# A fused attention and MLP kernel on one core: the SP queue's transfers pinned to program order through the attention, and the weight staging moved to later slots

## The chip, the core and the metric

The kernel runs on one core of a Trainium2 chip. The core has five engines that run their own instruction streams: TensorE (PE in the profile; PEld is its weight load), VectorE (DVE), ScalarE (ACT), GpSimd (POOL) and SyncE (SP). In this kernel SP computes nothing: it only issues DMA transfers, one after the other, and each transfer then runs on the core's 16 DMA engines. A transfer that is issued waits, at the head of SP's stream, until the data that it reads is there, and everything behind it waits as well.

The metric is the time of one execution in microseconds (us). Lower is better.

## What is computed

All in float32, with a sequence of 2048 tokens of 512 channels, 32 heads of 16 channels, a sliding window of 256 keys, and a hidden layer of 1792:

```python
x  = A_x
xn = layernorm(x)
q, k, v = split(xn @ A_wqkv)                       # 32 heads of 16
p  = softmax(mask(q @ k.T * 16 ** -0.5))           # causal, the last 256 keys
s  = (p @ v) @ A_wo
g  = silu(gelu(layernorm(xn) @ B_w1 + B_b1) @ B_w2 + B_b2)
return x + s * g
```

To keep float32 precision in TensorE's reduced format, the kernel splits operands into a high and a low part and sums three products (hi*hi, hi*lo, lo*hi).

## The kernel before, in words

**The slots.** The attention works through eight groups `n` of four heads, and each group through 16 blocks of 128 tokens. One step of this is a slot `t`; the loop at line 717 runs t from -16 to 128 and writes out what each engine gets, in order. In slot t, `prob_block` (line 456) computes the probabilities of group t // 16, block t % 16, in two halves: scores into the PSUM tile `stb`, exp by ScalarE into `pt`, masking by GpSimd. `pv_step` (line 477) multiplies the block before with the values (into `zo`) and copies the result into `oraw`. Twelve slots ahead of the probabilities, `max_block` (line 415) computes the same scores once more (into `xy` and `zo`) to find each row's maximum by VectorE; after every fourth block `max_rows` (line 440) sends 4 blocks of maxima through HBM (`mT_d`) into a spare row of the projection tile. The first pair of `stb` matmuls of slot 0 starts at 72.49 us, and every slot up to 115 has two such pairs, which is how slots are counted in the trace: slot 8 starts at 95.86, slot 9 at 98.88, slot 12 at 107.30, slot 13 at 116.19, slot 84 at 329.13 us.

**The fill work.** Between these steps TensorE gets pieces of other matmuls (the `fills`): projections of later groups (`job_qk`, line 244, and pairs of them, `pair_qk`, line 300, run by `tandem`, line 371), values, and the first hidden tiles of the MLP. A projection (n, c) covers group n and the c-th 512 tokens. When it is finished, its raw result is copied to `pjr`, ScalarE rounds it to the high part `sh`, GpSimd subtracts to get the low part (back into `pjr`), and SP sends four copies of the high part and two of the low part into the tile `qk`, which `max_block` and `prob_block` read. The first block of (n, c) is due in slot 16 n + 4 c - 12. The high part is made in slot `max(t + 1 + 2 * (c % 2), 16 * n - 28 + 4 * c)`, where t is the slot in which the projection ended, and the low part in the next slot that `quiet` (line 335) allows. For (1, 2) that is: ended in slot 8, high and low part in slot 9, due in slot 12.

**What sets the order.** `at(t, ...)` (line 582) puts a step into the middle of slot t. The class `Ordered` (line 32) wraps each engine, and pins each instruction behind the one before it on its engine, for all engines but SP. SP's instructions are put in order by the compiler's scheduler, from its own estimate of when data is ready; it may issue a transfer earlier or later than the program has it.

**The staging.** The MLP's weights are copied from the inputs into scratch HBM tensors `w_d` by 16 transfers of 512 KB (`stage_in`, line 533), put into slots 22, 24, ... 52 at line 670. They depend on nothing, and are read from slot 91 on (`fetch`, line 538).

**The MLP.** After the attention the loop over four chunks of 512 tokens does the hidden layer, the second layer, the output projection and the gate. It isn't touched.

Of the kernel before, what the change touches and what calls it, by code (L numbers as in the profile page):

```python
# [31 lines left out]
class Ordered:  # L32


    def __init__(self, tc, name):
        self.tc, self.name = tc, name

    def __getattr__(self, what):
        issue = getattr(getattr(self.tc.nc, self.name), what)

        def issued(*args, **kwargs):
            r = issue(*args, **kwargs)  # L42
            if self.name != "sync" and hasattr(r, "ins"):
                self.tc.keep_in_program_order(r)
            return r
        return issued
# [3 lines left out]
def mixer_kernel(ctx, tc, x, wqk, wv, wo, w1, b1, w2, b2, out):  # L50
# [22 lines left out]
    def copy_rows(dst, src):  # L73
        nc.sync.dma_start(dst.bitcast(F32), src.bitcast(F32))
# [169 lines left out]
    def job_qk(n, c):  # L244

        box = []
        ops = [(kt, a, b) for kt in range(KT) for a, b in PASSES]
        if not n and not c:
            ops.sort(key=lambda o: o[2])
        sl = slice(512 * c, 512 * (c + 1))  # L250

        def mm(i):
            if i == 0:
                box.append(fill_bank())
            kt, a, b = ops[i]
            nc.tensor.matmul(box[0], wqs[n][:, a, kt], big[:, b, kt, sl],
                             start=(i == 0), stop=(i == len(ops) - 1))

        def send(src, qk, tt):
            copy_rows(slots[n % 2][tt:P:4, qk, :, sl], src[64 * qk: 64 * qk + 64])  # L260

        def finish():
            hi = sgp.tile([P, 512], F32R, tag="sh", name=f"sh_{n}_{c}", bufs=2)
            raw = t2.tile([P, 512], F32, tag="t2", name=f"pjr_{n}_{c}")
            lo = raw.bitcast(F32R)
            nc.scalar.copy(raw, box[0])

            def high():
                nc.scalar.copy(hi, raw)
                if n >= 2:  # L270
                    copy_rows(slots[n % 2][3:P:32, 0, :, sl], slots[n % 2][7:P:32, 0, :, sl])
                for qk, tt in ((1, 0), (0, 0), (1, 2), (0, 1)):
                    send(hi, qk, tt)

            def low():
                (nc.gpsimd if n else nc.vector).tensor_tensor(lo, raw, hi.bitcast(F32), op=ALU.subtract)
                send(lo, 1, 1)
                send(lo, 0, 2)

# [20 lines left out]
    def pair_qk(n, c):  # L300
# [11 lines left out]
        def finish(ps, t, copy):  # L312
            hi = sgp.tile([P, 512], F32R, tag="sh", name=f"sh_{n}_{c}", bufs=2)
            raw = t2.tile([P, 512], F32, tag="t2", name=f"pjr_{n}_{c}")
            lo = raw.bitcast(F32R)
            copy(raw, ps)

            def high():
                nc.scalar.copy(hi, raw)
# [5 lines left out]
            def low():  # L325
                nc.gpsimd.tensor_tensor(lo, raw, hi.bitcast(F32), op=ALU.subtract)
                send(lo, 1, 1)
                send(lo, 0, 2)

            free = max(t + 1 + 2 * (c % 2), 16 * n - 28 + 4 * c)  # L330
            at(free, high)
            at(quiet(free), low)
        return 3 * KT, mm, finish

    def quiet(t):
# [20 lines left out]
    def pair_h(f):  # L356
# [5 lines left out]
        def finish(ps, t, copy):  # L362
            raw = t2.tile([P, 512], F32, tag="t2", name=f"hr_{f}")
            copy(raw, ps)
            if f < 4:
                soon[f] = raw
            else:
                nc.sync.dma_start(h_d[f - 6], raw)
        return 3 * KT, mm, finish

    def tandem(t0, t1, one, two, mid=None, back=None):
# [68 lines left out]
    def max_rows(n, c):  # L440

        mt = mts.pop((n, c))
        mh = small.tile([P, 2, 2, 2, 4], F32R, tag="mh", name=f"mh_{n}_{c}")
# [2 lines left out]
        mT = small.tile([P, 32], F32, tag="mT", name=f"mT_{n}_{c}")  # L446
        nc.vector.transpose(mT, mh.rearrange("p a l i b -> p (a l i b)").bitcast(F32))
        rows = mT_d[n, c]
        nc.sync.dma_start(rows.rearrange("r (i t) -> i r t", i=4), mT)
        nc.sync.dma_start(slots[n % 2][3:P:32, 0, :, 512 * c: 512 * (c + 1)].bitcast(F32),  # L450
                          rows.rearrange("(h p b) t -> h p (b t)", h=4, p=2))


    pts = {}
# [22 lines left out]
    def pv_step(n, qb, also=()):  # L477
# [11 lines left out]
            outs[0] = sgp.tile([P, 512], F32, tag="or", name=f"oraw_{n}_{qb}", bufs=2)  # L489
        nc.scalar.copy(outs[0][:, P * (qb % 4): P * (qb % 4 + 1)], otb)  # L490
        if qb % 4 == 3:
            nc.sync.dma_start(oT_d[n // 2, n % 2::2, :, P * (qb - 3): P * (qb + 1)], outs[0])


    mlp = {}
# [86 lines left out]
    def at(t, fn, *args):  # L582
        plan.setdefault(t, []).append((fn, args))

    fetch_wqk(0)
    fetch_wv(0)
    xs[1] = load_x(1, XE, "x")
# [349 lines left out]
```

## Time and profile before

| | |
|---|---|
| median of 3 runs | 791.07 us (789.85 to 793.46) |
| the profiled execution | 793.06 us |
| its span, first to last instruction | 791.4 us |
| mean granted TensorE clock | 0.992 |
| busy: PE, PEld | 756.2 us (96%), 587.8 us (74%) |
| busy: DVE, ACT, POOL | 484.6 us (61%), 373.0 us (47%), 313.5 us (40%) |
| the attention's slots 0 to 128 | 72.5 to about 452 us |
| DMA moved in all | 90.46 MB, 38.7% of the 16 engines' time on SP's queue |

How to read the profile: `out<-in` names the tile that an instruction writes and those that it reads. A wait is written `engine tile <- what ended the wait`. In a timeline the columns are start, length, engine and operation, a count, and in brackets the idle time ahead of it with its releaser. In a table of windows they are the stretch, its length, the busy time of each engine (with the number of instructions), the granted clock, the share of the DMA engines' time, and GB/s. On SP, the length of a group of transfers is the time to issue them, not the time until they land; landing times stand in the chain of waits, as `DMA out<-in`. All lines read L42 because the wrapper `Ordered` issues everything.

### The profile page before, as it was taken

To read this page: it belongs to the slowest core of one execution; us is meant where nothing else is said; L and a number is where in the kernel's file an instruction comes from. 1 tells how busy PE (TensorE), PEld (TensorE's weight loads), DVE (VectorE), ACT (ScalarE), POOL (GpSimd) and SP (SyncE) were. 2 spreads that over 40 slices of the span, in tenths; PEclk is the share of its full clock that TensorE was granted. 3 is DMA by queue.
4 is the path that set the end of the run, shared out by engine and by line. 5 is a ranking of instruction groups with operands and counts; after the bars stand their busy time and mean duration, and the time that the engine had idled before them with its cause. 6 is when DMAs were issued, how large, how long until landed. Compare 5 with 4: busy or idle time off the path is not lost.

```text
span 791.4 us, 18507 instructions
## 1 busy us (share of the span) xinstructions
PE 756.2 (96%) x7420; PEld 587.8 (74%) x7420; DVE 484.6 (61%) x751; ACT 373.0 (47%) x626; POOL 313.5 (40%) x586
## 2 busy tenths in 40 slices
PE   5999989999999999999999999999999999999997
PEld 4887656676668887666676777688888888888886
DVE  5786757787777678888974558733445235532343
ACT  4733746767776676777877834321122111221111
POOL 4101646657656554767766744320112011120101
PEclk9999989999999999999999999999999999999999
DMA  8965545555445312465623282530123011210011
GB/s 285 297 182 156 177 130 169 151 136 131 97 97 125 89 45 85 106 188 157 185 82 125 79 293 83 172 106 14 54 80 107 14 41 40 81 54 13 27 54 66
DMA packets 55061, 90.46 MB, mean 114 GB/s; under 512 B 10496, under 2 KB 14848, under 8 KB 54976
## 3 DMA queue, kind: packets, MB, share of 16 engines
q1 hardware_dynamic: 54976, 89.29, 38.7%
q8 instruction: 58, 0.95, 0.5%
q14 instruction: 27, 0.22, 0.1%
HBM read 44.05 MB, written 25.95 MB: 88 GB/s over the span
## 4 chain that ended last, share of the span: by engine, by line
PE 79%; DVE 8%; ACT 5%; DMA 3%; issue 2%; POOL 2%; SPq 1%; DVEq 0%; ACTq 0%; POOLq 0%
PE acc L42 16%; PE fb L42 16%; PE h L42 15%; PE zo L42 11%; PE stb L42 7%; PE s L42 6%; PE xy L42 5%; ACT pt L42 3%; PE pv L42 2%; DVE xy L42 2%; DVE mt L42 2%; POOL pt L42 1%; DVE xnT L42 1%; DMA qk<-sh 1%; DVE gl L42 1%
## 5 line engine op out<-in xcount | busy, mean ns | idle before, releaser
L42 POOL TENSOR_SCALAR_AFFINE_SELECT pt<-pt 128x256 f32<-128x256 f32 x480 | 196.1, 433 | 179.4 <-ACT pt L42 178.1
L42 ACT ACTIVATE pt<-stb 128x768 f32<-128x768 f32 (+1 forms) x244 | 189.0, 774 | 61.6 <-PE stb L42 53.2
L42 DVE TENSOR_REDUCE mt<-xy 128x4 f32<-128x1024 f32 (+1 forms) x128 | 152.6, 1192 | 4.4
L42 PE MATMUL acc<-w,gh 128*128 128x512 f32 x432 | 133.5, 390 | 1.0 <-DVE gh L42 1.0
L42 DVE COPY_PREDICATED xy<-upper,zo 128x512 f32<-128x512 int32 x112 | 77.6, 693 | 76.7 <-PE zo L42 75.9
L42 PE MATMUL fb<-xnT,wqb 64*128 64x512 f32 (+1 forms) x696 | 120.4, 410 | 0.6 <-DVE xnT L42 0.6
L42 ACT ACTIVATE g<-h,b1s 128x512 f32<-128x512 f32 x44 | 30.4, 691 | 189.9 <-PE h L42 189.9
L42 DVE CAST gh<-g 128x512 fp32r<-128x512 f32 x52 | 27.5, 529 | 137.9 <-PE acc L42 125.2
L42 PE MATMUL zo<-pt,vt 128*17 128x128 f32 x2880 | 104.4, 276 | 2.1 <-DVE xy L42 1.6
L42 PE MATMUL stb<-qk 64*128 64x384 f32 (+1 forms) x488 | 97.1, 393 | 7.3 <-ACT pt L42 5.8
L42 PEld LDWEIGHTS zo<-pt,vt 128*17 128x17 f32 x2880 | 67.8, 97 | 39.5 <-issue 18.2
L42 PEld LDWEIGHTS acc<-w,gh 128*128 128x128 f32 x432 | 80.9, 188 | 18.7 <-DVE gh L42 2.2
L42 PE MATMUL h<-xnT 128*128 128x512 f32 x320 | 92.0, 389 | 0.0
L42 PE MATMUL acc<-w,gl 128*128 128x512 f32 x216 | 84.8, 392 | 1.1 <-DVE gl L42 1.0
L42 PEld LDWEIGHTS stb<-qk 64*128 64x128 f32 x488 | 45.8, 184 | 52.5 <-ACT pt L42 41.3
L42 PEld LDWEIGHTS fb<-xnT,wqb 64*128 64x128 f32 (+1 forms) x696 | 67.5, 190 | 8.5 <-DVE xnT L42 1.0
L42 PEld LDWEIGHTS h<-xnT 128*128 128x128 f32 x320 | 60.1, 188 | 12.4
L42 PE MATMUL xy<-qk 64*128 64x256 f32 (+2 forms) x536 | 61.6, 304 | 6.6 <-DMA qk<-pjr 3.9
L42 PEld LDWEIGHTS xy<-qk 64*128 64x128 f32 x536 | 44.8, 187 | 17.0 <-issue 6.6
L42 PE MATMUL h<-yh,xnT 128*128 128x512 f32 x160 | 55.8, 389 | 0.0
L42 ACT COPY oraw<-zo 128x128 f32<-128x128 f32 x128 | 34.3, 268 | 39.0 <-PE zo L42 35.0
L42 POOL TENSOR_TENSOR or<-or,w 128x512 f32<-128x512 f32 x16 | 21.5, 1350 | 73.0 <-DMA or<-oT_d 65.1
(115 smaller groups left out, 962.7 us busy)
## 6 DMA issues: line engine op xcount, KB each, us to landing
qk<-sh SPq DMA_DIRECT2D x128, 128.0 KB
qk<-pjr SPq DMA_DIRECT2D x64, 128.0 KB
oT_d<-oraw SPq DMA_DIRECT2D x32, 256.0 KB
w_d<-in_w_dram SPq DMA_DIRECT2D x14, 512.0 KB
x<-in_x_dram SPq DMA_DIRECT2D x16, 256.0 KB
or<-oT_d SPq DMA_DIRECT2D x16, 256.0 KB
w<-rden_d SPq DMA_DIRECT2D x16, 256.0 KB
xo<-in_x_dram SPq DMA_DIRECT2D x16, 256.0 KB
```

The source lines that it names most:

```text
L42: r = issue(*args, **kwargs)
```

## The change

Four things change.

- **SP is pinned in the loop.** `Ordered` gets a switch; for SP it is on through the slot loop, so each transfer there is pinned behind the one before it in the program. Before and after the loop SP is free as it was.
- **Each transfer gets a place.** A new `behind(t, ...)` puts a step at the very end of slot t. The sends of a projection go behind the slot in which its high or low part is made; the two transfers of `max_rows` go into the middle of the next slot and behind the one after that; the store of `oraw` into the middle of the next slot; the `h_d` stores behind their slot.
- **(1, 2) is made earlier.** Its high part is rounded in slot 8, where the projection ends, and no longer in slot 9. Its low part stays in slot 9.
- **The staging moves** from slots 22 to 52, every second one, to behind slots 55 to 70, one in each.

```diff
     def __init__(self, tc, name):
         self.tc, self.name = tc, name
+        self.on = name != "sync"
...
             r = issue(*args, **kwargs)
-            if self.name != "sync" and hasattr(r, "ins"):
+            if self.on and hasattr(r, "ins"):
                 self.tc.keep_in_program_order(r)
```

```diff
@@ job_qk
             def high():
                 nc.scalar.copy(hi, raw)
-                if n >= 2:
-                    copy_rows(slots[n % 2][3:P:32, 0, :, sl], slots[n % 2][7:P:32, 0, :, sl])
+                behind(now[0], send_high)
+
+            def send_high():
                 for qk, tt in ((1, 0), (0, 0), (1, 2), (0, 1)):
                     send(hi, qk, tt)
 
             def low():
                 (nc.gpsimd if n else nc.vector).tensor_tensor(lo, raw, hi.bitcast(F32), op=ALU.subtract)
+                behind(now[0], send_low)
+
+            def send_low():
                 send(lo, 1, 1)
                 send(lo, 0, 2)
@@ pair_qk
-            free = max(t + 1 + 2 * (c % 2), 16 * n - 28 + 4 * c)
-            at(free, high)
-            at(quiet(free), low)
+            free = t if (n, c) == (1, 2) else max(t + 1 + 2 * (c % 2), 16 * n - 28 + 4 * c)
+            at(free, nc.scalar.copy, hi, raw)
+            behind(free, send_high)
+            free = quiet(max(free, t + 1))
+            at(free, lambda: nc.gpsimd.tensor_tensor(lo, raw, hi.bitcast(F32), op=ALU.subtract))
+            behind(free, send_low)
@@ pair_h
-                nc.sync.dma_start(h_d[f - 6], raw)
+                behind(t, nc.sync.dma_start, h_d[f - 6], raw)
@@ max_rows
-        nc.sync.dma_start(rows.rearrange("r (i t) -> i r t", i=4), mT)
-        nc.sync.dma_start(slots[n % 2][3:P:32, 0, :, 512 * c: 512 * (c + 1)].bitcast(F32),
-                          rows.rearrange("(h p b) t -> h p (b t)", h=4, p=2))
+        at(t + 1, nc.sync.dma_start, rows.rearrange("r (i t) -> i r t", i=4), mT)
+        behind(t + 2, nc.sync.dma_start, slots[n % 2][3:P:32, 0, :, 512 * c: 512 * (c + 1)].bitcast(F32),
+               rows.rearrange("(h p b) t -> h p (b t)", h=4, p=2))
@@ pv_step
-            nc.sync.dma_start(oT_d[n // 2, n % 2::2, :, P * (qb - 3): P * (qb + 1)], outs[0])
+            at(16 * n + qb + 2, nc.sync.dma_start, oT_d[n // 2, n % 2::2, :, P * (qb - 3): P * (qb + 1)], outs[0])
@@ the plan
+    ends = {}
+
+    def behind(t, fn, *args):
+
+        ends.setdefault(t, []).append((fn, args))
...
-        at(22 + 2 * k, stage_in, kind, j)
+        behind(55 + k, stage_in, kind, j)
@@ the slot loop
     end = 16 * NQ
+    nc.sync.on = True
     for t in range(-16, end + 1):
...
         if 0 <= m < end and m % 4 == 3:
-            max_rows(m // 16, m % 16 // 4)
+            max_rows(m // 16, m % 16 // 4, t)
+        for fn, args in ends.get(t, []):
+            fn(*args)
     for k in sorted(delayed):
         run(delayed[k])
+    for fn, args in plan[end + 1]:
+        fn(*args)
+    nc.sync.on = False
```

More of the change, by code (lines that the diff above doesn't have):

```diff
@@ L316, in finish, with send_high @@
             copy(raw, ps)
-            def high():
-                nc.scalar.copy(hi, raw)
+            def send_high():
                 if n >= 2:
@@ L323, in high, with send_low @@
                     send(hi, qk, tt)
-            def low():
-                nc.gpsimd.tensor_tensor(lo, raw, hi.bitcast(F32), op=ALU.subtract)
+            def send_low():
                 send(lo, 1, 1)
                 send(lo, 0, 2)
-            free = max(t + 1 + 2 * (c % 2), 16 * n - 28 + 4 * c)
-            at(free, high)
-            at(quiet(free), low)
+            free = t if (n, c) == (1, 2) else max(t + 1 + 2 * (c % 2), 16 * n - 28 + 4 * c)
[4 more added lines that the diff above has]
+            behind(free, send_low)
         return 3 * KT, mm, finish
@@ L438, in max_block, with max_rows @@
                                 axis=AX.X, op=ALU.max, negate=True)
-    def max_rows(n, c):
+    def max_rows(n, c, t):
         mt = mts.pop((n, c))
```

## The prediction

> **What bounds the kernel now.** The page first: TensorE is busy 96% of the span, and the chain that ended last runs through it.
>
> ```profile
> PE 756.2 (96%) x7420; PEld 587.8 (74%) x7420; DVE 484.6 (61%) x751; ACT 373.0 (47%) x626; POOL 313.5 (40%) x586
> ...
> PE 79%; DVE 8%; ACT 5%; DMA 3%; issue 2%; POOL 2%; SPq 1%; DVEq 0%; ACTq 0%; POOLq 0%
> ```
>
> So a change to the DMA order can win only what TensorE loses to transfers. The list of TensorE's own waits says how much that is:
>
> ```profile
> PE tr L42 <- ACT x L42: 10.4, 6, 6.7
> PE stb L42 <- ACT pt L42: 5.8, 16, 0.7
> PE xy L42 <- DMA qk<-pjr: 3.9, 1, 3.9
> ...
> PE xy L42 <- DMA qk<-sh: 0.2, 1, 0.2
> ```
>
> One wait of 3.9 us and one of 0.2 us. The first is in slot 12, where the first block of projection (1, 2) is due (TensorE's timeline; then windows over slots 9 to 11, slot 12, slot 13):
>
> ```profile
> 107.30 0.44 PE L42 MATMUL stb<-qk 64*128 64x384 f32 x2
> 111.60 0.80 PE L42 MATMUL xy<-qk 64*128 64x256 f32 x4 [3.86 <-DMA qk<-pjr]
> ```
> ```profile
> 98.88:107.30 8.42, 8.42 (x132) 6.05 (x132) 6.15 (x7) 6.54 (x11) 5.83 (x14) 1.00 0.58 154
> 107.30:116.19 8.89, 5.03 (x49) 3.48 (x45) 2.84 (x6) 1.89 (x3) 2.28 (x6) 0.66 0.49 140
> 116.19:119.47 3.28, 3.28 (x50) 2.48 (x46) 1.92 (x2) 1.89 (x3) 1.59 (x3) 0.89 0.12 11
> ```
>
> Slots 9 to 11 take 8.42 / 3 = 2.81 us each; slot 12 takes 8.89 with the same matmuls. The wait explains 3.9 of the excess of 6.08; the rest is the clock, granted at 0.66 in this window and still at 0.89 in the next. [...]
>
> Why the data was late stands in SP's timeline, its waits, and the chain:
>
> ```profile
> 91.10 1.92 SPq L42 DMA_DIRECT2D w_d<-in_w_dram  x3
> 96.67 0.59 SPq L42 DMA_DIRECT2D mT_d<-mT  x1
> ...
> 98.01 0.55 SPq L42 DMA_DIRECT2D w_d<-in_w_dram  x1
> 101.10 0.55 SPq L42 DMA_DIRECT2D qk<-mT_d  x1
> ...
> 102.24 0.54 SPq L42 DMA_DIRECT2D oT_d<-oraw  x1
> 102.88 3.72 SPq L42 DMA_DIRECT2D qk<-sh  x4
> 106.70 1.19 SPq L42 DMA_DIRECT2D qk<-pjr  x2
> ```
> ```profile
> SPq L42 <- DMA mT_d<-mT: 2.5, 1, 2.5
> ```
> ```profile
> 107.29 4.17 DMA qk<-pjr
> ```
>
> The scheduler has hoisted the staging (slots 22 on in the program) to before slot 9. Four staging transfers (512 KB each, by the page's list of issues) sit around `mT_d`; SP then waits 2.5 us for `mT_d` to land before it may read it back, until 101.10, and the sends of (1, 2) stand behind that. The last low part is issued at 107.29 and lands 4.17 us later, at 111.46; TensorE starts at 111.60. The data itself was ready long before (ScalarE's and GpSimd's timelines):
>
> ```profile
> 97.53 0.59 ACT L42 COPY pjr<-fb 128x512 f32<-128x512 f32 x1 [0.29 <-PE fb L42]
> 98.01 0.82 ACT L42 ACTIVATE pt<-stb 128x768 f32<-128x768 f32 x1
> ...
> 100.16 0.61 ACT L42 CAST sh<-pjr 128x512 fp32r<-128x512 f32 x1
> ```
> ```profile
> 101.07 1.29 POOL L42 TENSOR_TENSOR pjr<-pjr,sh 128x512 fp32r<-128x512 f32 x1
> ```
>
> **The change part by part.**
>
> *The wait of slot 12 goes.* Removed with it: 8.89 - 2.81 = 6.08 us, and in slot 13 what the slow clock cost, 3.28 x (1 - 0.89) = 0.36. Together **-6.4 us**. What is late next decides how much stays, so I work out the new order, with this row for the time of an issue:
>
> ```profile
> L42 SPq DMA_DIRECT2D qk<-sh x128: 526/592/1470, 22.3 to 388.4; - x128
> ```
>
> In slot 8 the rounding moves ahead of the second exp, to about 98.1, so the high part is ready at 98.7, and SP, pinned, has only `mT_d` ahead (96.67). Four sends take 4 x 0.6 us (the median, 592 ns), to 101.2. Slot 9 has the store of `oraw` (0.54) and the read-back of the maxima (0.55), to 102.3, and no staging ahead, so `mT_d` has landed. The low part ends at 101.07 + 1.29 = 102.4, or 102.9 with the delay of the next item; its second send goes out at 103.5. Landing times in the chain of waits range from 2.35 us undisturbed, over the 4.17 above, to 4.94 when the sends stand close behind an `oraw` store (SP's timeline, then the chain):
>
> ```profile
> 130.40 0.52 SPq L42 DMA_DIRECT2D oT_d<-oraw  x1
> ```
> ```profile
> 133.54 4.94 DMA qk<-sh
> ...
> 150.01 2.35 DMA qk<-sh
> ```
>
> That is 105.9 to 108.4. Slot 12's `xy` would start 0.3 us into the slot, at 107.30 + 0.3 + 0.5 = 108.1. So the residual wait is 0 to 0.3 us; I take 0, by the row nearest to it (4.17: 107.7).
>
> *The rounding in slot 8.* The second exp of slot 8 started at 98.01; behind a rounding of 0.61 us it starts at about 98.55. Slot 9's first matmuls already wait for it:
>
> ```profile
> 98.88 0.45 PE L42 MATMUL stb<-qk 64*128 64x384 f32 x2 [0.37 <-ACT pt L42]
> ```
>
> Nothing covers this: **+0.55 us** (0 to 0.61). Slot 9 loses the same rounding, but there TensorE is the slower one, so nothing comes back.
>
> *The start.* In slot -15 four `xn_d` stores now precede the two low sends of (0, 0):
>
> ```profile
> 24.88 1.19 SPq L42 DMA_DIRECT2D qk<-pjr  x2
> 26.11 2.04 SPq L42 DMA_DIRECT2D xn_d<-x  x4
> ```
> ```profile
> 30.07 0.44 PE L42 MATMUL xy<-qk 64*128 64x128 f32 x4
> ```
>
> The second low send moves from 25.5 to about 25.5 + 2.0 = 27.5 and lands at 29.9 (2.35) to 31.7 (4.17); it is due at 30.07. That is 0 to 1.6 us; in its favour no staging follows close behind any more. I take **+0.2**.
>
> *Other sends.* Projection (2, 0) ends the 0.2 us wait listed above; with `oraw` stored a little earlier than now I count it away: **-0.2**. The next tight one is (6, 0), due in slot 84:
>
> ```profile
> 322.07 0.55 SPq L42 DMA_DIRECT2D oT_d<-oraw  x1
> 323.12 1.17 SPq L42 DMA_DIRECT2D qk<-pjr  x2
> ...
> 329.42 0.34 PE L42 MATMUL xy<-qk 64*128 64x128 f32 x4
> ```
>
> Last send 323.7, plus 4.94 is 328.6, 0.8 us before its use. The new order adds the row-clearing copy (0.6) ahead of the four high sends, but moves the read-back (0.53) behind the low ones; the low sends wait for GpSimd, not for SP. I count 0. Only (1, 3), with its low part in slot 13 and due in slot 16, and (2, 0), 17 and 20, have as little room, three slots; the projections after them have six or more. The maxima are read seven slots after they are made and now leave SP about two slots later: 0.
>
> *The staging in slots 55 to 70.* Sixteen issues of 0.6 us on a queue that computes nothing. Bandwidth is the question (windows over the staging now, and over the slots that get it):
>
> ```profile
> 74.00:82.00 8.00, 7.87 (x67) 4.70 (x68) 5.29 (x6) 5.96 (x10) 5.53 (x13) 1.00 0.84 298
> 250.00:290.00 40.00, 39.27 (x698) 33.18 (x688) 28.38 (x39) 26.37 (x46) 22.35 (x53) 1.00 0.38 90
> ```
>
> 298 / 0.84 = 355 GB/s at full share, so 16 x 0.524 MB = 8.4 MB take 23.6 us of all engines; over 16 slots of 3.0 us that is a share of 0.49 on top of 0.38, 0.87. It fits, and no projection is due before slot 68. I count 0; if a backlog held up the loads of slot 74, due in slot 77, the wait could be some 4 us. Elsewhere SP's order stays close to what the scheduler chose: 0, within 1 us.
>
> **Sum:** -6.4 + 0.55 + 0.2 - 0.2 = -5.85, which I round to -5.5, since the small unknowns (residual wait, backlog) only add. The profiled execution would take 793.06 - 5.5 = 787.6. It was 2.0 us above the median, 791.07, so the median goes to **785.5 us**. Its own range: the low ends of the unknowns (no cost in slot 8 and at the start, 1 us won elsewhere, and a base 1.2 us lower, as the fastest run shows) give 782.5; 787.2 at the high end.
>
> **The rivals.**
>
> *A short wait stays, and the clock falls all the same.* [...] In slot 9 the store now stands right ahead of the low sends, and the sends of the trace that stand behind such a store landed last of the three rows, after 4.94 us, which agrees. If the low part of (1, 2) lands 1 us later than that, at 109.5, the wait is 1.4; with as much half clock as now (6.4 - 3.9 = 2.5 us) 3.9 of the 5.85 go, and the median is 789. Against it: the window with the longest waits on `pt` (1.35 us in all) keeps the clock at 1.00:
>
> ```profile
> 130.00:140.00 10.00, 8.65 (x114) 6.00 (x114) 8.77 (x13) 7.69 (x15) 8.19 (x16) 1.00 0.52 135
> ```
>
> Chance **0.15**.
>
> *Nothing moves.* If the scheduler's order was no cause, and some transfer ends slot 12 as late as now, or the gain is paid back in the tail after the loop, where SP is free: 791 +- 1. For it: ends of waits are inferred. Against: SP's wait on `mT_d` between two staging transfers is in the rows. **0.13**.
>
> *Slower: the head of the line.* A pinned transfer whose data is late holds all behind it. The price of one missed first use is known: 6.4 us. The margin at slot 84 is 0.8 us, and (1, 3) in slot 16 and (2, 0) in slot 20 are built alike. [...] Against: SP's issues through these slots are some 14 in four slots, 8 of 12 us. **0.12**.
>
> **How the numbers follow.** 0.60 for the forecast (782.5 to 787.2). The range takes in the short wait up to 790: 782.5 to 790.0. A difference under 0.5%, 4.0 us, is about what a measurement of this kernel can't tell from no change, so faster means below 787.1: 0.60 and a part of the first rival, 0.65. Same: the rest of it and the second, 0.21. Slower: 0.14.
>
> **What would show it.** Right: no `PE xy <- DMA qk<-pjr` over 0.5 us in TensorE's waits, clock 1.00 between 100 and 130 us, slot 12 about 2.8 us long, the sends of (1, 2) at 98.7 and 103, no `w_d` before 230 us, and 0.5 us more of `PE stb <- ACT pt` in slot 9. Wrong: a DMA wait in front of `xy` in slots -12, 16, 20 or 84, DVE waiting for `y` near 300 us, or a longer stretch after the loop.

## The result, and the profile after

| | before | after |
|---|---|---|
| median of the comparison's runs | 791.44 us (788.57 to 795.87) | **788.84 us** (787.35 to 791.22) |
| ratio of the runs | | **0.9962**, 95% [0.9949, 0.9975] |
| the profiled execution, its span | 793.06, 791.4 us | 788.93, 787.2 us |
| mean granted TensorE clock | 0.992 | 0.996 |

The kernel after is 0.38% faster, 3.0 us by the ratio and 2.6 us by the medians. The forecast was 5.6 us. All lines read L43 now.

The page of the kernel after, first and fourth part. TensorE works 3.8 us less for the same 7420 matmuls; 2.3 us of that lie in slots 9 to 13 (16.73 to 14.40 us in the windows below), where the half clock is gone. Transfers hold 2% of the chain in place of 3%.

```profile
PE 752.4 (96%) x7420; PEld 584.8 (74%) x7420; DVE 483.9 (61%) x751; ACT 372.4 (47%) x626; POOL 311.7 (40%) x586
...
PE 80%; DVE 8%; ACT 5%; issue 3%; DMA 2%; POOL 1%; SPq 0%; DVEq 0%; ACTq 0%; POOLq 0%
```

TensorE's waits in the kernel after. The 3.9 us are gone, but two transfers are still waited for, 1.7 and 0.7 us, and the wait for `pt` has a longest case of 1.0 us.

```profile
PE stb L43 <- ACT pt L43: 6.0, 15, 1.0
...
PE xy L43 <- DMA qk<-pjr: 1.7, 1, 1.7
...
PE xy L43 <- DMA qk<-sh: 0.7, 1, 0.7
```

TensorE's timeline in the kernel after places them: the first is in slot -12, the 1.0 us at the start of slot 9, the third in slot 12.

```profile
31.44 0.44 PE L43 MATMUL xy<-qk 64*128 64x128 f32 x4 [1.67 <-DMA qk<-pjr]
...
100.87 0.44 PE L43 MATMUL stb<-qk 64*128 64x384 f32 x2 [1.01 <-ACT pt L43]
...
110.39 0.50 PE L43 MATMUL xy<-qk 64*128 64x256 f32 x4 [0.70 <-DMA qk<-sh]
```

To see where the time went, cut both traces at the same instructions. Windows of the kernel before over slots 0 to 8, slots 9 to 13, and slot 14 to the last `stb` of the attention; then the same of the kernel after:

```profile
72.49:98.88 26.39, 25.85 (x330) 17.19 (x330) 19.09 (x26) 19.49 (x32) 15.94 (x36) 1.00 0.66 201
98.88:119.47 20.59, 16.73 (x222) 12.01 (x222) 10.91 (x14) 10.32 (x17) 9.70 (x22) 0.83 0.47 125
119.47:451.83 332.36, 321.99 (x4944) 235.53 (x4942) 249.82 (x348) 236.23 (x414) 213.72 (x458) 1.00 0.45 120
```
```profile
73.81:100.86 27.05, 25.80 (x330) 17.20 (x330) 19.75 (x26) 20.06 (x33) 15.87 (x36) 1.00 0.36 83
100.86:115.97 15.11, 14.40 (x223) 10.37 (x223) 10.36 (x13) 9.79 (x16) 9.70 (x22) 1.00 0.54 127
115.97:448.51 332.54, 322.26 (x4943) 235.59 (x4941) 249.74 (x348) 235.78 (x414) 212.89 (x458) 1.00 0.53 142
```

The second column is the length. The starts and lengths give the whole balance of the two profiled executions:

| stretch | before | after | difference |
|---|---|---|---|
| up to slot 0 | 72.49 | 73.81 | +1.32 |
| slots 0 to 8 | 26.39 | 27.05 | +0.66 |
| slots 9 to 13 | 20.59 | 15.11 | -5.48 |
| slot 14 to the end of the attention | 332.36 | 332.54 | +0.18 |
| the MLP, to the end of the span | 339.6 | 338.7 | -0.9 |

The change edits nothing in the last row's code, so its own balance is -3.3 us. The staging's new place shows in the DMA columns: slots 0 to 8 fall from 201 to 83 GB/s, the long stretch rises from 120 to 142, and it costs TensorE nothing there.

SP's timeline in the kernel after (start, time to issue). The order is the one that was written: the sends of (1, 2) go out at 100.13 and 104.54 with no staging near, and at the start the two low sends of (0, 0) stand behind the four `xn_d` stores.

```profile
24.70 2.84 SPq L43 DMA_DIRECT2D xn_d<-x  x4
27.63 1.21 SPq L43 DMA_DIRECT2D qk<-pjr  x2
...
98.02 0.52 SPq L43 DMA_DIRECT2D mT_d<-mT  x1
100.13 3.00 SPq L43 DMA_DIRECT2D qk<-sh  x4
103.23 0.55 SPq L43 DMA_DIRECT2D oT_d<-oraw  x1
103.90 0.55 SPq L43 DMA_DIRECT2D qk<-mT_d  x1
104.54 1.20 SPq L43 DMA_DIRECT2D qk<-pjr  x2
```

The chain of waits in the kernel after holds the send of slot -12: issued 27.63, landed 3.22 us later, at 30.85. TensorE went on at 31.44; the second of the pair, issued 0.6 us behind the first, is not in the chain.

```profile
27.63 3.22 DMA qk<-pjr
```

So four questions are open: what the two waits that stayed are worth (e1 to e3), whether the earlier rounding did anything (e7, e9), whether it was the staging's place or the kept order (e5, e6, e8, e11, e12), and what makes transfers land late at all (e2, e10, e13). The theory at this point: staging beside the maxima and the sends of (1, 2) made the stall, and moving it away cured it. The rivals: the written order did; or the early rounding did; or the store of `oraw` is the root.

### The profile page after: what moved, and what is told of

Same layout as the page of the kernel before. It is cut to its first block, busy times and chain, and to the rows that moved or that the text cites. A ratio compares the mean times of both kernels' runs of the same rounds, so it can differ in the third digit from the quotient of the medians.

```text
span 787.2 us, 18487 instructions
## 1 busy us (share of the span) xinstructions
PE 752.4 (96%) x7420; PEld 584.8 (74%) x7420; DVE 483.9 (61%) x751; ACT 372.4 (47%) x626; POOL 311.7 (40%) x586
## 4 chain that ended last, share of the span: by engine, by line
PE 80%; DVE 8%; ACT 5%; issue 3%; DMA 2%; POOL 1%; SPq 0%; DVEq 0%; ACTq 0%; POOLq 0%
PE acc L43 17%; PE fb L43 16%; PE h L43 15%; PE zo L43 12%; PE stb L43 7%; PE s L43 6%; PE xy L43 5%; ACT pt L43 3%; DVE xy L43 2%; DVE mt L43 2%; PE pv L43 2%; DVE xnT L43 1%; POOL pt L43 1%; PE yt L43 1%; DVE gl L43 1%
## 5 line engine op out<-in xcount | busy, mean ns | idle before, releaser
L43 POOL TENSOR_SCALAR_AFFINE_SELECT pt<-pt 128x256 f32<-128x256 f32 x480 | 195.2, 431 | 176.6 <-ACT pt L43 175.2
L43 ACT ACTIVATE pt<-stb 128x768 f32<-128x768 f32 (+1 forms) x244 | 188.6, 773 | 58.1 <-PE stb L43 48.4
L43 DVE TENSOR_REDUCE mt<-xy 128x4 f32<-128x1024 f32 (+1 forms) x128 | 152.6, 1192 | 4.4
L43 PE MATMUL acc<-w,gh 128*128 128x512 f32 x432 | 133.5, 390 | 0.3 <-DVE gh L43 0.2
L43 DVE COPY_PREDICATED xy<-upper,zo 128x512 f32<-128x512 int32 x112 | 77.6, 693 | 71.8 <-PE zo L43 69.8
L43 ACT ACTIVATE g<-h,b1s 128x512 f32<-128x512 f32 x44 | 30.3, 688 | 190.0 <-PE h L43 190.0
L43 PE MATMUL fb<-xnT,wqb 64*128 64x512 f32 (+1 forms) x696 | 117.7, 404 | 0.8 <-DVE xnT L43 0.6
L43 DVE CAST gh<-g 128x512 fp32r<-128x512 f32 x52 | 28.4, 546 | 137.6 <-PE acc L43 124.8
L43 PE MATMUL zo<-pt,vt 128*17 128x128 f32 x2880 | 103.7, 275 | 2.5 <-DVE xy L43 1.9
L43 PE MATMUL stb<-qk 64*128 64x384 f32 (+1 forms) x488 | 96.6, 392 | 7.5 <-ACT pt L43 6.0
L43 PEld LDWEIGHTS zo<-pt,vt 128*17 128x17 f32 x2880 | 67.6, 97 | 39.6 <-issue 17.9
L43 PEld LDWEIGHTS acc<-w,gh 128*128 128x128 f32 x432 | 80.8, 188 | 18.0 <-DVE gh L43 1.5
L43 PE MATMUL h<-xnT 128*128 128x512 f32 x320 | 92.0, 389 | 0.0
L43 PE MATMUL acc<-w,gl 128*128 128x512 f32 x216 | 84.6, 392 | 1.3 <-DVE gl L43 1.2
L43 PEld LDWEIGHTS stb<-qk 64*128 64x128 f32 x488 | 45.6, 183 | 52.2 <-ACT pt L43 41.2
L43 PEld LDWEIGHTS fb<-xnT,wqb 64*128 64x128 f32 (+1 forms) x696 | 65.5, 186 | 8.2 <-DVE xnT L43 0.9
L43 PEld LDWEIGHTS h<-xnT 128*128 128x128 f32 x320 | 60.1, 188 | 12.5
L43 PE MATMUL xy<-qk 64*128 64x256 f32 (+2 forms) x536 | 61.3, 302 | 4.9 <-DVE mt L43 2.3
L43 PE MATMUL h<-yh,xnT 128*128 128x512 f32 x160 | 55.7, 389 | 0.0
L43 PEld LDWEIGHTS xy<-qk 64*128 64x128 f32 x536 | 44.1, 185 | 15.6 <-DVE mt L43 6.5
L43 ACT COPY oraw<-zo 128x128 f32<-128x128 f32 x128 | 34.1, 267 | 38.3 <-PE zo L43 33.8
L43 POOL TENSOR_TENSOR or<-or,w 128x512 f32<-128x512 f32 x16 | 20.7, 1296 | 74.9 <-DMA or<-oT_d 65.6
```

## Experiments

All ratios are against runs of the kernel before on the same chip, and the kernels were measured on several chips; so medians of two kernels compare less well than their ratios, and a ratio is not the quotient of the two medians. The stretches are those of the table above, from the one profiled execution of each kernel.

| kernel | median, us | ratio, 95% | slot 0 starts | slots 0 to 8 | slots 9 to 13 | slots 62 to 74 |
|---|---|---|---|---|---|---|
| before | 791.4 to 792.4 | | 72.49 | 26.39 | 20.59 | 38.10 |
| after | 788.84 | 0.9962 [0.9949, 0.9975] | 73.81 | 27.05 | 15.11 | 38.07 |
| e1_start | 788.25 | 0.9946 [0.9929, 0.9962] | 72.24 | 27.05 | 15.18 | 38.12 |
| e2_store16 | 788.58 | 0.9954 [0.9938, 0.9970] | 74.47 | 27.05 | 14.26 | 38.11 |
| e3_both | 787.15 | 0.9934 [0.9915, 0.9952] | 71.17 | 27.07 | 14.27 | 38.13 |
| e7_late12 | 789.06 | 0.9958 [0.9941, 0.9974] | 75.53 | 26.65 | 14.27 | 38.11 |
| e9_both_late12 | 786.68 | 0.9918 [0.9891, 0.9945] | 72.28 | 26.41 | 14.28 | 38.11 |
| e6_early_stage | 789.62 | 0.9965 [0.9946, 0.9983] | 74.01 | 27.06 | 17.40 | 38.12 |
| e8_nopin | 793.16 | 1.0009 [0.9990, 1.0027] | 73.38 | 27.04 | 20.49 | 38.11 |
| e12_stage22 | 789.07 | 0.9976 [0.9956, 0.9996] | 73.35 | 27.06 | 14.66 | 38.09 |
| e5_stage_only | 795.97 | 1.0037 [1.0015, 1.0058] | 72.04 | 26.41 | 14.73 | 49.02 |
| e11_readback | 806.55 | 1.0180 [1.0156, 1.0204] | 75.28 | 27.06 | 14.52 | 53.51 |
| e10_stage16 | 785.94 | 0.9924 [0.9905, 0.9943] | 72.72 | 26.41 | 14.28 | 38.08 |
| e13_store_only | 786.75 | 0.9941 [0.9927, 0.9955] | 71.66 | 26.43 | 14.28 | 38.09 |

### The two waits that stayed: e1_start, e2_store16, e3_both

e1_start puts the `xn_d` stores one slot later, behind the low sends of (0, 0):

```diff
-        at(-15, nc.sync.dma_start, xn_d[4 + i], xs[1][i])
+        at(-14, nc.sync.dma_start, xn_d[4 + i], xs[1][i])
```

> The changed kernel, with the four xn_d stores of slot -15 put into slot -14, behind the two low sends of (0, 0). Theory (the stores ahead of these sends make slot -12 wait): the 1.7 us wait of xy for pjr near 30 us goes, slot 0 starts 1.3 us earlier (about 72.5), and the time falls by 1.3 us against the changed kernel, to about 787.5 where that has 788.8. Rival (the DMA engines are full at the start in any order, by the xs loads): the wait stays over 1 us and the time stays within 0.4 us of 788.8.

Measured: 788.25 us, 0.9946. The wait of slot -12 is gone (TensorE's timeline of e1_start), and slot 0 starts 1.57 us earlier than in the kernel after. The median fell by 0.6 us, less than the 1.3 expected; by the ratios it is 1.3 us, but the two intervals overlap. The wait in slot 12 is about as before this edit, 0.76 us.

```profile
29.82 0.44 PE L43 MATMUL xy<-qk 64*128 64x128 f32 x4
```

e2_store16 stores `oraw` in another shape. The store has 4 outer rows of 32 in the kernels before and after, because the four heads of a group lie two apart in `oT_d`; here they lie next to each other, so that the outermost dimension has 128 rows (the expectations write "16 outer rows" for this shape, and put the old one on few, or four, DMA engines; that is the author's estimate, and what the traces show of it are the semaphore updates given under e13_store_only, four late ones for the old shape and 16 for this one). The bytes are the same; the rows of `wo` are fed in the matching order.

```diff
-            at(..., nc.sync.dma_start, oT_d[n // 2, n % 2::2, :, ...], outs[0])
+            at(..., nc.sync.dma_start, oT_d.rearrange("g (b j) r t -> g b (j r) t", b=2)[n // 2, n % 2, :, ...], outs[0])
...
-        "wo": np.asarray(A_wo).reshape(4, 2, 4, DH, D).transpose(0, 2, 1, 3, 4).reshape(4, P, D)
+        "wo": np.asarray(A_wo).reshape(4, P, D)
```

> The changed kernel, with the scratch tensor of the attention's output laid out so that the store of oraw has 128 outer rows and not 4 by 32 (the heads' order changes, and wo is laid out to match). Theory (the store of slot 9 sits on few DMA engines and holds up the low sends of (1, 2) behind it): the store lands in about 3 us and not 6, the low sends of slot 9 in under 3.2 us and not 5.0, and the 0.7 us wait of slot 12 goes: -0.7 to -0.9 us against the changed kernel, about 788.0. Rival (the sends are late because SP issues them late, at 104.5): they land as late as now and the time stays at 788.8 within 0.4.

Measured: 788.58 us, 0.9954. The wait of slot 12 is gone; slots 9 to 13 take 14.26 us in place of 15.11. In e2_store16's timeline of TensorE, `xy` follows `stb` without a gap:

```profile
109.90 0.44 PE L43 MATMUL stb<-qk 64*128 64x384 f32 x2
110.19 0.50 PE L43 MATMUL xy<-qk 64*128 64x256 f32 x4
```

That also settles whose wait the 0.7 us were. The list names a high send of (1, 3), issued at 108.34 in the kernel after; e2 issues the same send at 109.00, its `xy` runs at 110.19 without waiting, and 1.19 us is too short for it to land (1.94 in the chain of the kernel after). So the label only marks the last landing by the profile, and what slot 12 waited for was the low part behind the `oraw` store. The trace also keeps each update of the semaphores, from which the landings are read, and they agree: in the kernel after the last update for the second low part comes at 110.15 us, 5.0 us behind its issue, and TensorE starts at 110.39; in e2_store16 it comes 2.35 us behind its issue. The median moved by 0.3 us only. In the profiled execution the start was worse (a wait of 2.01 us and half clock behind it); whether that hides the 0.85 us in the other runs isn't shown.

e3_both has both edits.

> Both edits: stores of xn_d in slot -14 and the store of oraw with 128 outer rows. Theory: both waits go, -2.0 to -2.3 us against the changed kernel, about 786.6, with no wait of xy for a DMA over 0.3 us. Rival (what the forecast missed lies in the kernel before, whose median pays less for the clock than the profiled execution): under 0.8 us from the changed kernel.

Measured: 787.15 us, 0.9934. Slot 0 starts at 71.17, slots 9 to 13 take 14.27. Both waits were real, and both went or shrank with the cause named: slot 12 doesn't wait, and 0.33 us are left in slot -12. Together they are worth 1.7 us against the kernel after by the medians, 2.2 us by the ratios, where 2.0 to 2.3 were expected.

### The early rounding: e7_late12, e9_both_late12

```diff
-            free = t if (n, c) == (1, 2) else max(t + 1 + 2 * (c % 2), 16 * n - 28 + 4 * c)
+            free = max(t + 1 + 2 * (c % 2), 16 * n - 28 + 4 * c)
```

> The changed kernel, but the high part of (1, 2) is rounded in slot 9 again, as before. Theory: the 0.6 us that slot 9 lost to the rounding in slot 8 come back, but the four high sends now go out in slot 9 behind the oraw store and ahead of the low sends, so the low sends leave 2.4 us later and slot 12 waits some 2.5 to 3 us and not 0.7: +1.5 to +2 us against the changed kernel, 790.5, and more where the clock falls. Rival (the early rounding is worth nothing): -0.6 us, 788.2.

Measured: 789.06 us, 0.9958. My expectation was wrong. Slot 12 does not wait at all, and slots 9 to 13 take 14.27. SP's timeline of e7_late12 fits with the store as the cause: with the sends later, the store of `oraw` is 4.8 us ahead of the low sends, no longer 1.3 us. The last semaphore updates of the two come 2.9 us behind their issue, where the second took 5.0 us in the kernel after.

```profile
102.31 0.51 SPq L43 DMA_DIRECT2D oT_d<-oraw  x1
102.93 0.53 SPq L43 DMA_DIRECT2D qk<-mT_d  x1
104.09 2.93 SPq L43 DMA_DIRECT2D qk<-sh  x4
107.12 1.19 SPq L43 DMA_DIRECT2D qk<-pjr  x2
```

Slots 0 to 8 get 0.40 us back. The median didn't move. In the profiled execution the start took the gain back, with a wait of 3.17 us for the send of (0, 0), so that slot 0 started at 75.53; whether it did so in the other runs isn't shown. e9_both_late12 is e3_both with this edit:

> The kernel after with three edits: the xn_d stores one slot later (as e1_start), the store of oraw in a shape of 16 outer rows (as e2_store16; the feed of wo is ordered to match), and the high part of (1, 2) rounded in slot 9 again (as e7_late12). Theory (with the staging away and the store on more engines the sends of (1, 2) have room even with the later rounding, which costs nothing there): no wait in slot 12, slot 9 without its 0.6 us, no wait in slot -12; 0.5 us under e3_both, so 786.5. Rival (the later rounding takes the last of the room): the wait of slot 12 returns with 0.5 to 1.5 us and the time is that of e3_both or 1 us more, 787.2 to 788.

Measured: 786.68 us, 0.9918: no wait for a transfer in slots -12 or 12, slots 0 to 8 back at 26.41. In the traces the early rounding costs 0.6 us in slots 0 to 8 and buys nothing; the medians of e3 and e9 lie 0.5 us apart, within the spread of their runs.

### The staging's place: e6_early_stage, e8_nopin, e12_stage22

e6_early_stage keeps the order but puts four of the 16 transfers about where the scheduler had them:

```diff
-        behind(55 + k, stage_in, kind, j)
+        behind({0: 5, 1: 5, 2: 5, 3: 8}.get(k, 55 + k), stage_in, kind, j)
```

> The kernel after, with four of the 16 staging transfers brought forward in the written order: three behind slot 5 and one behind slot 8, about where the scheduler had put them in the kernel before; the other twelve stay in slots 55 to 70. Theory (staging beside the maxima and the sends of (1, 2) is the cause): the store of the maxima lands late, SP waits for it, the low sends of (1, 2) land 1 to 3 us later, the wait in slot 12 grows from 0.7 us to 2 to 4 us, and with half clock for a part the time is 790 to 793. Rival (it was the order of SP's issues, not the traffic): the wait stays under 1 us and the time at 788.8 +- 0.5.

Measured: 789.62 us, 0.9965. The wait in slot 12 grew, less than expected, to 1.59 us, and the half clock came with it. Timeline of TensorE, then windows over slot 12 up to the wait, the wait itself, and two stretches behind it (the clock is the third number from the end):

```profile
111.47 0.51 PE L43 MATMUL xy<-qk 64*128 64x256 f32 x4 [1.59 <-DMA qk<-pjr]
```
```profile
105.00:109.90 4.90, 4.89 (x80) 3.12 (x76) 3.92 (x6) 3.68 (x7) 2.99 (x9) 1.00 0.50 110
109.90:111.47 1.57, 0.00 (x0) 0.03 (x1) 0.53 (x2) 0.81 (x1) 0.88 (x3) 1.00 0.63 178
111.47:114.90 3.43, 3.43 (x42) 2.53 (x42) 1.92 (x2) 0.81 (x1) 0.77 (x3) 0.66 0.60 161
114.90:118.50 3.60, 3.60 (x56) 2.56 (x48) 1.92 (x2) 1.89 (x3) 1.82 (x4) 0.85 0.11 12
```

Slots 9 to 13 take 17.40 us, 3.1 more than the 14.28 without any wait. Half of that is the wait, half the clock. That is one execution, and the slowest of its twelve (792.55 us); the ratio of 0.9965 is about that of the kernel after, so what the usual run loses by the early staging isn't shown.

e8_nopin is the kernel after without the line `nc.sync.on = True`, so that the scheduler orders SP again.

> The kernel after with the same text of the program, slots 55 to 70 for the staging and sends behind their slots, but SP's instructions free for the scheduler again. The scheduler takes five staging transfers up to right behind the low sends of (0, 0), near 28 us, and the others to before slot 12. Theory (what helps is that the staging really leaves SP only in slots 55 to 70, which needs the kept order): staging is back beside the sends of (1, 2), the wait of slot 12 returns with 2 to 4 us, the time is 790 to 792.5. Rival (early rounding and the place in the program are enough): wait under 1 us, 788.8 or, without the start's wait, 787.5.

Measured: 793.16 us, 1.0009. The scheduler pulls the staging back in front of slot 9 in spite of its new place in the text, and slots 9 to 13 take 20.49 us, as before the change. The time is a little over the 790 to 792.5 expected. Without the kept order the rest of the change gains nothing.

e12_stage22 gives the staging the slots of the old text, with the order kept:

```diff
-        behind(55 + k, stage_in, kind, j)
+        behind(22 + 2 * k, stage_in, kind, j)
```

> The kernel after with the staging in the slots that the text of the kernel before gives it, one transfer of 512 KB behind every second slot from 22 to 52, the order kept. Theory (any place outside slots 5 to 12 does, as long as the order is kept and the read-back stands behind the sends): no new wait in slots 22 to 55, 788.8 +- 0.6. Rival (slots 22 to 52 have more sends of their own and less room than 55 to 70): waits of xy on pjr or of zo on oraw of 1 us or more in slots 24 to 56, 790 or more.

Measured: 789.07 us, 0.9976, with no new wait in slots 22 to 55. By this trace slots 55 to 70 are nothing special; the ratio is a little nearer to 1 than that of the kernel after, with overlapping intervals.

### What the kept order is for: e5_stage_only, e11_readback

e5_stage_only takes the kernel before and moves only the staging, each transfer pinned behind its slot 55 to 70; everything else on SP stays with the scheduler.

```diff
-        nc.sync.dma_start(w_d[kind][:, sl], {...}[kind][:, sl])
+        tc.keep_in_program_order(nc.sync.dma_start(w_d[kind][:, sl], {...}[kind][:, sl]))
...
-        at(22 + 2 * k, stage_in, kind, j)
+        staged[55 + k] = (kind, j)
...
+        if t in staged:
+            stage_in(*staged[t])
```

> The kernel before with one part of the change alone: each of the 16 staging transfers keeps the program's order and stands behind the slot 55 to 70 that it has in the kernel after; everything else on SP is ordered by the scheduler as before, the rounding of (1, 2) stays in slot 9, and the xn_d stores stay behind the low sends of (0, 0). Theory (the staging ahead of the read-back of the maxima made the stall of slot 12, and nothing else did): the wait of xy on pjr in slot 12 falls from 3.9 us to 0.7 or less, the clock there is 1.00, no wait in slot -12 and no rounding ahead of an exp in slot 8, so the time is under that of the kernel after by the 0.6 to 2 us that these two cost it: 786.5 to 788. Rival (the written order of the sends, or the early rounding, is needed too): a wait of 2 us or more stays in slot 12, with part of the half clock, and the time is 789.5 to 791.

Measured: 795.97 us, 1.0037, slower than before. Slot 12 did as the theory said: slots 9 to 13 take 14.73, with a last wait of 0.28 us. But slots 62 to 74 take 49.02 us in place of 38.10. The stall moved along with the staging. Windows over these slots in the kernel after and in e5_stage_only:

```profile
259.36:297.43 38.07, 37.28 (x662) 31.32 (x658) 28.20 (x40) 25.81 (x45) 20.53 (x50) 1.00 0.70 213
```
```profile
256.22:305.25 49.03, 41.46 (x663) 34.35 (x660) 28.17 (x40) 25.60 (x45) 20.55 (x50) 0.90 0.61 182
```

In e5_stage_only the DMA engines moved less per us than in the kernel after (182 against 213 GB/s), so what they can move in all was not the limit. TensorE's waits, SP's waits between 250 and 300 us, SP's timeline and the chain of e5_stage_only:

```profile
PE zo L42 <- ACT oraw L42: 6.8, 2, 3.7
```
```profile
SPq L42 <- DMA mT_d<-mT: 14.9, 3, 6.9
```
```profile
250.88 0.58 SPq L42 DMA_DIRECT2D mT_d<-mT  x1
251.56 0.60 SPq L42 DMA_DIRECT2D qk<-qk  x1
259.12 0.55 SPq L42 DMA_DIRECT2D qk<-mT_d  x1
259.73 0.55 SPq L42 DMA_DIRECT2D w_d<-in_w_dram  x1
260.38 2.52 SPq L42 DMA_DIRECT2D qk<-sh  x4
262.94 0.56 SPq L42 DMA_DIRECT2D oT_d<-oraw  x1
```
```profile
262.94 8.54 DMA oT_d<-oraw
```

Read it in this order. The scheduler puts the read-back of the maxima almost directly behind their store. The store lands late, behind staging and an `oraw` store, so SP stands from 252.2 to 259.1 with everything else behind it. The next `oraw` store therefore goes out late, and lands 8.54 us later, at 271.48. There are two `oraw` buffers; ScalarE may not fill the next one before that, and TensorE's `zo` waits for ScalarE.

e11_readback tests this link alone. It is the kernel after, with the read-back of the maxima put back behind their store:

```diff
-        behind(t + 2, nc.sync.dma_start, slots[...][3:P:32, 0, :, ...], rows...)
+        at(t + 1, nc.sync.dma_start, slots[...][3:P:32, 0, :, ...], rows...)
```

> The kernel after with one line back: the read-back of the maxima is issued right behind their store, in slot t+1, instead of behind the sends of slot t+2. Theory (this place of the read-back is what the kept order is needed for): SP stands 4 to 7 us for each of the maxima of slots 62 to 72, the sends and the store of oraw behind it come late, TensorE waits for oraw there by 3 to 7 us, half clock follows, and the time is 793 to 797 while slots 0 to 60 stay as in the kernel after. Rival (some other difference to the scheduler's order made the stall of e5_stage_only): no wait on oraw, 788.8 +- 0.7.

Measured: 806.55 us, 1.0180, 17.7 us over the kernel after by the medians, more than the 4 to 8 expected. SP's waits of e11_readback, its window over slots 62 to 74 and TensorE's waits there:

```profile
SPq L43 <- DMA mT_d<-mT: 96.4, 32, 7.6
```
```profile
260.45:313.96 53.51, 43.42 (x662) 35.85 (x658) 28.31 (x40) 25.42 (x45) 20.60 (x50) 0.84 0.60 185
```
```profile
262.79 0.44 PE L43 MATMUL zo<-qk 64*128 64x128 f32 x4 [1.71 <-ACT oraw L43]
...
280.03 0.69 PE L43 MATMUL zo<-qk 64*128 64x128 f32 x4 [3.89 <-ACT oraw L43]
...
297.05 0.69 PE L43 MATMUL zo<-qk 64*128 64x128 f32 x4 [3.46 <-ACT oraw L43]
```

SP waits for each of the 32 sets of maxima, 96.4 us in all (9.7 us in the kernel after). With the order kept, SP can't fill that time with something else, as the scheduler's order could (44.4 us of such waits in e5_stage_only). The head of projection (6, 0) in slot 84, whose margin the prediction put at 0.8 us, gives way too, with a wait of 1.92 us. So the one line that puts the read-back behind the sends is what makes a kept order bearable.

### The root: e10_stage16, e13_store_only

The late transfers of slots 12 and 62 to 74 all stand near an `oraw` store. e10_stage16 is e5_stage_only with the store of e2_store16:

> The kernel before with the staging alone moved to slots 55 to 70 (as e5_stage_only) and the store of oraw in a shape of 16 outer rows (as e2_store16; the feed of wo is ordered to match). Theory (e5_stage_only lost its 6 us of slot 12 again in slots 66 to 72 because the scheduler puts the read-back of the maxima right behind their store, and that store landed 8 us late behind a store of oraw on four DMA engines and the staging): with the store of oraw on all engines the maxima land in 2 to 5 us, TensorE's waits on oraw in slots 66 to 72 fall from 6.8 us to 2 or less, and with no wait at the start and in slot 12 the time is 785.5 to 788. Rival (the staging traffic alone holds the maxima up): TensorE's waits on oraw stay at 5 us or more and the time at 792 or more.

Measured: 785.94 us, 0.9924. TensorE's waits on `oraw` are gone, slots 62 to 74 take 38.08 us, with the scheduler's order and the read-back still directly behind its store (SP's longest wait for the maxima: 4.5 us, where it was 7.8).

Last, e13_store_only: the kernel before, the store's shape changed, and nothing else. The staging stays hoisted.

> The kernel before with the store of oraw in a shape of 16 outer rows and nothing else (the feed of wo is ordered to match); the staging stays where the scheduler puts it, most of it before slot 12. Theory (slot 12 is late because staging and the maxima meet on SP and on the DMA engines, not because of the store): TensorE waits 2 to 4 us on pjr in slot 12 as before, and the time is 790.5 to 792. Rival (the store on four engines is the common root of all the stalls): the wait falls under 1 us and the time to 786 to 788.

Measured: 786.75 us, 0.9941. My theory fell and its rival held: slot 12 does not wait, slots 9 to 13 take 14.28 us, and the clock stays at 1.00, with all the staging where it was. SP's timeline of e13_store_only, to be put beside that of the kernel before in the prediction; the first line is the `oraw` store of the kernel before, which stands a little ahead of the lines shown there:

```profile
89.84 0.55 SPq L42 DMA_DIRECT2D oT_d<-oraw  x1
```

```profile
89.04 0.38 SPq L42 DMA_DIRECT2D oT_d<-oraw  x1
89.51 0.58 SPq L42 DMA_DIRECT2D qk<-qk  x1
90.14 1.85 SPq L42 DMA_DIRECT2D w_d<-in_w_dram  x3
95.87 0.59 SPq L42 DMA_DIRECT2D mT_d<-mT  x1
...
98.08 0.55 SPq L42 DMA_DIRECT2D qk<-mT_d  x1
```

The store of the maxima stands behind the same three staging transfers. From its issue to the issue of the read-back it is now 2.21 us (95.87 to 98.08); in the kernel before it was 4.43 (96.67 to 101.10).

The updates of the semaphores show the queue. In the kernel before, the `oraw` store gets one update 0.96 us behind its issue and four more between 6.10 and 6.97 us; in e13 it gets 16, the last at 3.09 us. The first staging transfer behind it gets twelve updates by 4.06 us and the last four at 5.95 to 7.12 us in the kernel before; in e13 all 16 come by 4.38 us. The store of the maxima gets four late ones as well: the last at 4.42 us in the kernel before, at 2.20 us in e13. Read as one update for each engine, which is the author's estimate, the old store and the store of the maxima ran on four of the core's 16 DMA engines and not on all, and the four that held up the staging were behind by what the old store had given them. The trace doesn't name the four of the maxima, but their lateness fits with the same ones. The queue behind the `oraw` store was what delayed the maxima, and the staging made that queue long. Either remedy cures slot 12: staging away (e5), or the store in the shape whose last update comes at 3.09 us in place of 6.97 (e13). Neither ingredient alone makes the stall of 3.9 us; the store without the staging leaves 0.70 us in the kernel after.

The traces show the number, four late updates against 16, and the runs the effect: same bytes, other outer dimension, and the stalls vanish, in slot 12 (slots 9 to 13 take 14.26 us in e2 and 14.28 in e13) and in slots 62 to 74 (38.08 us in e10, 49.02 in e5). How the number of updates follows from the outer rows, 4 against 128, isn't shown; no run tried a third shape of this store.

Two kernels beat the kernel after clear of the intervals: e9 at 0.9918 and e10 at 0.9924. e3 (0.9934) and e13 (0.9941) come out ahead of it too, but their intervals touch its own. All four overlap, and by the medians e10 leads and e9 and e13 are level, so which is best stays open. e13 needs neither the kept order nor the move of the staging.

## Why the prediction was half right

The sign and the place held, and of the mechanism the wait with its clock and SP's order; the size was about twice the measured one. The measured 788.84 us lies in the range of 782.5 to 790.0, but only in the part that was added for the first rival: the forecast's own range ended at 787.2. Since that rival's price was for a half clock in slot 12 that didn't come, it is in part luck that the range held. Of the prediction's own signs of being right, the clock, the order of the sends and the absence of `w_d` before 230 us (the first is at 237.1) came true, but slot 12 took 3.67 us, not about 2.8; of its signs of being wrong, the wait in slot -12 did. Step by step:

- **The wait of slot 12, -6.4 with its clock.** It went. Slots 9 to 13 fall to 14.26 to 14.28 us in the six kernels whose slot 12 doesn't wait at all (e2, e3, e7, e9, e10, e13); the forecast amounts to 20.59 - 6.4 = 14.19. The size was right.
- **Why the data was late.** Half right. SP's order around `mT_d` was read correctly, but the staging was taken for the whole cause. e13 keeps the staging and loses the wait.
- **Residual wait of slot 12, 0 (0 to 0.3).** Wrong: 0.70, and slots 9 to 13 at 15.11, 0.8 over 14.28. The step took the row of 4.17 us as the nearest. The row of 4.94 us, with the sends close behind an `oraw` store, was the one that fitted, and the first rival said so. The second low part took 5.0 us to land, and by e2 it is this store that held it.
- **The rounding in slot 8, +0.55.** Right: slots 0 to 8 are 0.66 longer, and the wait for `pt` at slot 9 rose from 0.37 to 1.01. The step took the earlier rounding as given and didn't ask whether it was needed; by e7 and e9 it wasn't.
- **The start, +0.2 (0 to 1.6).** Mis-sized: +1.32. The four stores took 2.84 us to issue, not 2.04, and the send went out at 28.2 us (27.63 plus half of 1.21), not at 27.5. Six kernels whose low sends follow the stores (after, e2, e6, e7, e11, e12) start slot 0 at 73.35 to 75.53 us, and seven in which they don't (before, e1, e3, e5, e9, e10, e13) at 71.17 to 72.72; the means lie 2.3 us apart. (e8, where the scheduler put staging behind those sends, waited 2.3 us there as well.) This was the largest error in a term.
- **Other sends, -0.2.** The wait is gone from the list, but the stretch from slot 14 on is 0.18 us longer, not shorter.
- **The staging in slots 55 to 70, 0; the maxima two slots later, 0.** Right as results: the long stretch is unchanged, with the clock at 1.00. But the two steps hang together, and the prediction did not see it. It asked when projections were due; the danger was SP waiting at the read-back and the two `oraw` buffers. What the second step priced at 0 is a line whose removal costs 17.7 us (e11).
- **The base.** The forecast carried the 2.0 us by which the profiled execution before was over its median to the kernel after, whose profiled execution was 0.1 us over its own. And 0.9 us of the profiled difference lies in the MLP, where the change does nothing. That accounts for 1.9 us of the 3.3 by which the median missed; the terms above account for most of the rest: 1.1 (start), 0.8 (residual wait), 0.4 (other sends) and 0.1 (slot 8), less the 0.35 that were rounded off and the 0.9 of the MLP.

Of the rivals, "a short wait stays and the clock falls" named the `oraw` store as the cause and 789 us as the time. The time fits, but not as it was put: the clock stayed at 1.00 behind the 0.70 us. It took e6's 1.59 us to see that mechanism whole. "The head of the line" didn't happen in the kernel after; its mechanism, a late transfer that holds all behind it, is what e5 and e11 paid for, 10.9 and 15.4 us in slots 62 to 74, but by the `oraw` buffers and not by the projections that it named (of those only slot 84 waited, 1.92 us in e11).

What stays open: why the start's wait differs so much from trace to trace with the same order (1.53 to 3.17 us). In these six traces the `xy` of slot -12 starts between 30.47 and 31.61 us and TensorE is ready for it between 28.40 and 29.97 us, so more of the spread comes from when TensorE gets there than from the sends; what sets either isn't shown. Open is also how much of the half clock a usual execution of the kernel before pays, since its own runs have mean clocks from 0.990 to 0.998.

## What to carry to other kernels

When several transfers on one queue land late, look at what stands ahead of them, and at the shape of it before its place: in these runs a store with 4 outer rows, whose last update came 6.97 us behind its issue (3.09 us with 128 rows), delayed what followed it, and changing the order moved the wait or shortened it (0.70 us left in slot 12, 10.9 us in slots 62 to 74 of e5), while changing the shape ended it. If a queue is pinned to program order, put every transfer that reads back what the queue has just stored as far behind that store as its use allows; here one line that didn't cost 17.7 us (e11). Moving traffic out of a hot stretch needn't be free in the stretch that gets it, even where bandwidth is left (slots 62 to 74 of e5 take 49.02 us in place of 38.10, at 182 GB/s where the kernel after moved 213): ask for each buffer and each wait on that queue what happens when a landing takes 8.54 us, as in e5, in place of 2.35.

## What the runs showed of the hardware

- **Half clock after short waits, not every time.** TensorE stood 1.59 us in e6 and was granted 0.66 in the 3.4 us after it. The start of e2 (2.01 us) was followed by 0.69 in the next 3.6 us, but that of the kernel after (1.67 us) and of e12 (1.53 us) by 1.00. Over all 14 traces, TensorE's waits for a transfer or for `oraw` from slot -12 to the end of the attention fall into three lots: five of 0.23 to 0.76 us, none with half clock in the 7 us behind it; nine of 1.53 to 2.33 us, four with it (1.59, 1.71, 2.01, 2.20) and five without (1.53, 1.64, 1.67, 1.92, 2.33); seven of 3.12 to 3.89 us, all with it. The clock's record holds only 1.00 and 0.50, the latter in stretches of 3.4 or 6.8 us in this part of the kernel (in the kernel before 6.83 us from 110.10 on, around the end of the wait of 3.86 us); values between are means over a window. What decides between the four and the five of the middle lot isn't shown; so in this kernel a wait of 1.6 us has to be priced with a possible half clock.
- **A store's shape is felt by its neighbours.** The issue of the `oraw` store fell from 0.54 to 0.38 us on SP with the other shape, which is nothing; the gain was in the transfers behind it, 0.85 us in slot 12 (e2 against the kernel after), 6.3 us there in e13 against the kernel before, and 10.9 us in slots 62 to 74 (e10 against e5).
